# Feed-forward weights repacked into scratch DRAM by their first users, in a two-layer recurrent-memory transformer kernel

## The chip, the cores and the metric

One core of one Trainium2 chip runs the whole program. The metric is the device time of one execution in microseconds (us); lower is better. Times quoted as a median are of plain runs. The profile is of one further execution, with its own time.

## The reference, cut to what matters

Two layers of the same form run after each other on 2048 tokens of width 576. Attention goes through the tokens in 64 segments of 32, with 8 memory tokens handed from each segment to the next, so the segments of one layer can't be done at once. The feed-forward part has no such chain.

```
def _B_ref(x, w1, w3, w2):          # w1, w3: 576 x 4608, w2: 4608 x 576, bfloat16
    gate = jnp.einsum('bsd,df->bsf', x, w1)
    up = jnp.einsum('bsd,df->bsf', x, w3)
    h = _silu(gate) * up
    return jnp.einsum('bsf,fd->bsd', h, w2)

# A: 32 heads of 128, per segment: 8 memory tokens + 32 tokens, masked softmax, output projection;
#    the first 8 rows of a segment's output are the next segment's memory
x = x + _A_ref(_layernorm(x, axis=-1), A_mem0, A_Wq, A_Wk, A_Wv, A_Wo, A_seg_len)
x = x + _B_ref(_layernorm(x, axis=-1), B_w1, B_w3, B_w2)
# ... and the same two lines a second time, with the same weights
```

Both layers use the same weights.

## The kernel before

**Steps.** The program has 72 steps. Step `t` does segment `t` of the first layer and segment `t - 8` of the second, side by side where both exist, so the middle 56 steps are alike. A step goes through four groups of eight heads: projections (tiles `HT`, `W`, `QKT`), scores, softmax on VectorE and ScalarE (`SME`, `STAT`), the probabilities `PB`, their transposition to `PTS`, the product with `V`, and the output projection `WO`. In the middle steps the transposition is a DMA (`ptd`, the rows `PTS<-PB`). The tile `PB` has to be zeroed by GpSimd (`pb_zero`) before two of the four groups of each step.

**Jobs.** After every four steps a `job(j)` does the feed-forward part for 128 tokens of the first layer and 128 of the second (`ents` holds one or two of them). Its matrix products are laid between the attention of the next four steps. The hidden width of 4608 is cut into 18 units of 256 (`NPR = 18`), taken in pairs. Unit `pr` needs two blocks of weights: `W13` (256 columns of w1 and of w3: 576 KB) and `W2C` (256 rows of w2: 288 KB). The attention's weights stay in SBUF, so there is room for two `W13` slots and two `W2C` slots only, and every job loads all its units from the inputs again. That makes 302 loads of a unit: 18 in each of the jobs 0 to 15 and 14 in job 16. The last job's weights come in eight large pieces into the room that the attention's weights leave free (`tail_load`).

**Layouts.** w1 and w3 lie in DRAM as 576 rows of 4608, so a unit's `W13` is gathered from 1152 runs of 512 bytes. `load_w13` takes four DMAs for that: two of 128 x 4 x 256 elements and two of 64 x 256 (the last 64 of the 576 rows). `load_w2` is one DMA of 256 runs of 1152 bytes.

**Order.** TensorE's order is a string of letters (`ORDER`). The order on the other queues comes from `plan`, which goes through the nodes with estimated durations (a load: bytes / `dma_bw` and a latency) and picks at each point what can start first. A `Slot` is taken when its load is planned and comes free when all its `users` have released it. The emitted program keeps this order on each engine, and semaphores guard the data. All loads and the transpositions are issued by SyncE (SP) in one queue. GpSimd (POOL) zeroes `PB`, takes one power per layer norm (`LNS`), loads `XR` and stores the output.

Helpers record all operations, so many have one line: 653 is TensorE's, 666 ScalarE's, 669 VectorE's, 672 SP's plain loads, 687 GpSimd's DMAs, 1092 the zeroing of `PB`, 841 the power, 1095 the transposition.

Of the kernel before, what the change touches and what calls it, by code (L numbers as in the profile page):

```python
# [7 lines left out]
BF = mybir.dt.bfloat16  # L8
# [5 lines left out]
P = 128  # L14
# [225 lines left out]
    ustep, mode_pen, hor, wait, bulk, ff_split, last_win, tail_at = 0.0315, 0.1194, 0.0162, 0.141, 0.02, False, 2.5, -1.5  # L240


def make_nodes(em, nseg, pools, o=Opt, dma_bw=230e3, load_bw=400e3):

    ngrp = nseg // 4
    nodes = []
# [224 lines left out]
        return node("DVE", dve(576), em.post_add(li, g, xr[g], b[0]), deps=[d], prio=prio, rel=b, name="POSTa")  # L471

    last_up = []
    last_reads = [], []
    kept = {}

    def job(j):

        ents = [(0, j)] if 0 <= j < ngrp else []
        if 0 <= j - 2 < ngrp:  # L480
            ents.append((1, j - 2))
        if not ents:
            return
        s0 = 4 * j + 4 if j < ngrp else 4 * j - 4 + LAG
        ne = len(ents)
        last = s0 >= nst
        wr = []
        prev_ff = [] if last else list(last_up)
        cost = ewh(640)
        for (bi, g) in reversed(ents):  # L490
            pa = post(bi, g)
            wr += ln_nodes("F", xr[g], Slot("xn"), [pa], s0, [((lambda bi: lambda b: em.xtb_write(em.col(bi, g), b))(bi), cost, prev_ff)])
        w2_last = {}

        def finish(g, es):

            xn = Slot("xn")
            c = node("ACT", 0.574, em.fin_cast(xr[g], xn), deps=es, prio=s0 + LAG - 4.2, acq=[xn], rel=[xr[g]], name="fin")
            node("SWD", 1.0, em.store(g, xn), deps=[c], prio=s0 + LAG - 4.2, rel=[xn], lat=3.0, name="store")

        tail = None
        if last:
            v_done, qk_done = last_reads
            me = steps[nst - 1]
            rest = me["WO3"]
            pace = [(0, 2, me["SC1"]), (0, 3, me["PV0"]), (0, 4, me["WO1"]), (0, 1, me["WO1"]), (1, 2, me["PV3"]), (1, 3, rest), (1, 4, rest), (1, 1, rest),
                    (2, 2, rest), (2, 3, rest), (2, 4, rest), (2, 1, rest), (3, 2, rest), (3, 3, rest), (3, 4, rest), (3, 1, rest)]
            size = {1: kb(128, 8 * 576), 2: kb(128, 4 * 1024), 3: kb(128, 4 * 1024), 4: kb(128, 1024)}
            parts = {}
            for k, (i, what, after) in enumerate(pace):  # L510
                free = v_done if what == 1 else qk_done[4 * i:4 * i + 4]
                parts.setdefault(i, []).append(load("tail", size[what], s0 - 3.0 + 0.01 * k, em.tail_load(i, what, after), deps=free + [after]))
            tail = [parts[i // 2] for i in range(8)]

        npp = NPR // 2
        split = HELD if j == ngrp else 0
        own = ents
        if last:
            prev = [(1, own[0][1] - 1)]
            todo = [(pp, prev, 0.2 * pp - 1.0) for pp in range(HELD)] + [(pp, own, at) for at, pp in enumerate([npp - 1] + list(range(npp - 1)))]  # L520
        else:
            todo = [(pp, own, at) for at, pp in enumerate(range(split, npp))]
        for pp, ents, at in todo:
            mids, w2s, htts, lds = [], [], [], []
            stays = last and pp == npp - 1
            ne = len(ents)
            mm = (128 * ne / 2.4 + 2.5) / 1000
            for pr_ in (2 * pp, 2 * pp + 1):
                prio = s0 + o.ff + (o.win if s0 + 4 < nst else o.last_win) * (2 * at + pr_ % 2) / NPR
                if stays:  # L530
                    w13, w2 = kept[pr_]
                    ld = []
                    w2s.append(w2)
                elif last:
                    w13 = w2 = None
                    ld = tail[pp]
                else:
                    keep = s0 < nst <= s0 + 4 and pp == npp - 1
                    w13, w2 = Slot("w13", users=2 + keep), Slot("w2", users=ne + keep)
                    kept[pr_] = w13, w2  # L540
                    ld = [node("DMA", kb(1152, 256) / dma_bw, em.load_w13(pr_, w13), prio=prio - 1, acq=[w13], lat=2.3, name="W13")]
                    lds.append(node("DMA", kb(256, 576) / dma_bw, em.load_w2(pr_, w2), prio=prio - 0.99, acq=[w2], lat=2.2, name="W2l"))
                    w2s.append(w2)
                b = banks()
                if ne == 2 or pr_ % 2 == 0:
                    htt = Slot("htt", users=ne)
                at_ = em.htt_at(ents, pr_)
                rel13 = [w13] if w13 else []
                wd = ld if ents is not own else wr + ld
                fm = node("PE", 16 * mm, em.ffn_up(ents, pr_, w13, b, last and not stays, False), deps=wd, prio=prio, mode="full/col",  # L550
                          acq=b + [htt], rel=rel13, name="FF", wide=0.01)
                ff = node("PE", 2 * mm, em.ffn_up(ents, pr_, w13, b, last and not stays, True), deps=wd, prio=prio + o.fft, mode="row",
                          acq=b + [htt], rel=rel13, name="FFt")
                a = node("ACT", actc(256 * ne), em.ffn_tanh(ents, b, htt, at_), deps=[fm, ff], prio=prio - 0.5, name="tanh")
                c = node("DVE", 2 * dve(256 * ne) + 0.12, em.ffn_mul(ents, b, htt, at_), deps=[a], prio=prio - 0.5, rel=b, name="mul")
                last_up[:] = [fm, ff]
                mids.append(c)
                htts.append((htt, at_))
            for (bi, g) in ents:
                b = banks()  # L560
                used = list({id(h): h for h, _ in htts}.values()) + w2s
                at_bi = em.col(bi, g) * P if ne == 2 else 0
                if last and at == npp - 1:
                    d = node("PE", 4 * 0.1225, em.ffn_down(at_bi, pp, htts, w2s, b, True, (0,)), deps=mids[:1], prio=prio + o.w2,
                             mode="full/col", acq=b, name="W2b", wide=0.003)
                    mids = mids[1:] + [d]
                d = node("PE", (4 if last and at == npp - 1 else 8) * 0.1225, em.ffn_down(at_bi, pp, htts, w2s, b, last and not stays, (1,) if last and at == npp - 1 else (0, 1)),
                         deps=mids + lds, prio=prio + o.w2, mode="full/col", acq=b, rel=used, name="W2b" if bi else "W2", wide=0.005)
                if last and at == npp - 1:
                    xn = Slot("xn")  # L570
                    for h in (0, 1):
                        e_ = node("DVE", dve(288), em.fin_add(g, h, xr[g], xn, b[h]), deps=[d], prio=prio + o.w2, acq=[xn], rel=[b[h]], name="W2a")
                        node("SWD", 1.0, em.store_half(g, h, xn), deps=[e_], prio=s0 + LAG - 4.2, lat=2.0, name="store")
                    return
                es = [node("DVE", dve(288), em.ffn_add(g, h, xr[g], b[h]), deps=[d], prio=prio + o.w2, rel=[b[h]], name="W2a")
                      for h in (0, 1)]
                w2_last[bi] = es
                if last and ents is not own and pp == HELD - 1:
                    finish(g, es)
        for (bi, g) in own:  # L580
            if bi == 0:
                ht_set(1, g, ln_nodes("L1", xr[g], Slot("xn"), w2_last[0], s0 + LAG - 4.2, ht_writes(1, g)))
            elif not split:
                finish(g, w2_last[1])
# [43 lines left out]
class Emitter:  # L628
# [140 lines left out]
    def load_x(self, g, xr):  # L769
        return lambda n: self.swdma(self.T.XR[:, xr.i, :], self.a.x[g * P:(g + 1) * P, :])  # L770

    def load_w13(self, pr, w13):
        def f(n):
            fa = pr * 2 * P
            W = self.T.W13[:, w13.i]
            for kind, wd in ((0, self.a.w1), (1, self.a.w3)):
                self.dma(W[:, 4 * kind:4 * kind + 4], wd[0:4 * P, fa:fa + 2 * P].rearrange("(c p) f -> p c f", p=P))
            for kind, wd in ((0, self.a.w1), (1, self.a.w3)):
                self.dma(W[kind * R64:(kind + 1) * R64, 8], wd[4 * P:D, fa:fa + 2 * P])
        return f  # L780

    def load_w2(self, pr, w2):
        fa = pr * 2 * P
        return lambda n: self.dma(self.T.W2C[:, w2.i], self.a.w2[fa:fa + 2 * P, :].rearrange("(b p) d -> p b d", p=P))

    def tail_load(self, i, what, after):

# [529 lines left out]
def kernel(  # L1317
# [60 lines left out]
    T.W13 = sp.tile([P, pools["w13"], NCH, 2 * P], BF, name="W13")  # L1378
    T.W2C = sp.tile([P, pools["w2"], 2, D], BF, name="W2C")
    T.HTT = sp.tile([P, pools["htt"], 2, 2 * P], BF, name="HTT")  # L1380
    T.M0 = T.XTB[:].rearrange("p a b -> p (a b)")[:, 0:D]

    T.banks = [pp.tile([P, 512], F32, name=f"bank{i}") for i in range(pools["bank"])]
# [62 lines left out]
```

## Time and profile before

| | |
|---|---|
| median of 3 runs | 2625.83 us (2620.28 to 2628.71) |
| the profiled execution | 2624.02 us, of which the span is 2622.2 us |
| granted TensorE clock | 0.999 |
| TensorE (PE) busy | 2567.1 us, 98% of the span |
| VectorE (DVE), ScalarE (ACT), GpSimd (POOL) busy | 77%, 48%, 7% |
| SP's DMA queue (q1) | 353.23 MB, 52.5% of the time of 16 DMA engines |

How to read it: "A <- B" in a row of waits means that A stood idle until B had ended, with the total in us, the number of times and the longest; PEld is TensorE's loading of weights, and an engine's name with a q is its instruction queue. A row of DMA issues gives the size of one DMA and the median time from its issue to the landing of its data. In the program's names `W<-in_B_w_dram` stands for the loads of `W13` and of the last job's weights alike (the profile leaves numbers out of names).

### The profile page before, as it was taken

To read this page: it belongs to the slowest core of one execution; us is meant where nothing else is said; L and a number is where in the kernel's file an instruction comes from. 1 tells how busy PE (TensorE), PEld (TensorE's weight loads), DVE (VectorE), ACT (ScalarE), POOL (GpSimd) and SP (SyncE) were. 2 spreads that over 40 slices of the span, in tenths; PEclk is the share of its full clock that TensorE was granted. 3 is DMA by queue.
4 is the path that set the end of the run, shared out by engine and by line. 5 is a ranking of instruction groups with operands and counts; after the bars stand their busy time and mean duration, and the time that the engine had idled before them with its cause. 6 is when DMAs were issued, how large, how long until landed. Compare 5 with 4: busy or idle time off the path is not lost.

```text
span 2622.2 us, 131462 instructions
## 1 busy us (share of the span) xinstructions
PE 2567.1 (98%) x58447; PEld 2205.6 (84%) x58498; DVE 2009.5 (77%) x5145; ACT 1266.8 (48%) x3743; POOL 196.1 (7%) x253
## 2 busy tenths in 40 slices
PE   6999999999999999999999999999999999999998
PEld 4788888888888888888888888888888888888887
DVE  4778777787787688777867877786787778777877
ACT  2655453544545354454535445453544545445553
POOL 1100000000001000000000000010000000010000
PEclk9999999999999999999999999999999999999999
DMA  9064746565464656555465655546465554554447
GB/s 326 4 181 126 193 103 154 126 152 136 126 139 115 148 128 153 135 126 141 115 148 128 155 133 127 144 109 151 128 156 132 126 143 112 128 146 129 123 131 258
DMA packets 680217, 369.58 MB, mean 141 GB/s; under 512 B 233592, under 2 KB 669824, under 8 KB 679008
## 3 DMA queue, kind: packets, MB, share of 16 engines
q1 hardware_dynamic: 675968, 353.23, 52.5%
q8 instruction: 457, 7.49, 1.2%
q0 software_dynamic: 3024, 6.93, 0.9%
q10 hardware_dynamic: 656, 1.02, 0.2%
q14 instruction: 112, 0.92, 0.1%
HBM read 304.95 MB, written 2.36 MB: 117 GB/s over the span
## 4 chain that ended last, share of the span: by engine, by line
PE 90%; DMA 4%; DVE 3%; SPq 1%; issue 1%; ACT 1%; ACTq 0%; DVEq 0%
PE bank L653 90%; DMA PTS<-PB 2%; DMA W<-in_B_w_dram 1%; SPq L672 1%; DVE STAT L669 1%; DVE PB L669 1%; DVE SME L669 1%; DMA WV<-in_A_Wv_dram 0%; DVE HTT L669 0%; DMA W<-in_A_Wk_dram 0%; ACT V L666 0%; DVE V L669 0%; PE bank L663 0%; DMA W2C<-in_B_w_dram 0%; ACT HT L666 0%
## 5 line engine op out<-in xcount | busy, mean ns | idle before, releaser
L653 PEld LDWEIGHTS <-W 128*128 128x128 bf16 (+2 forms) x32096 | 1252.3, 100 | 121.3 <-issue 66.1
L653 PE MATMUL bank<-HT,W 128*128 128x80 bf16 (+3 forms) x23040 | 792.9, 197 | 9.6 <-ACT HT L666 5.4
L653 PE MATMUL bank<-XTB,W 128*64 128x256 bf16 (+5 forms) x9056 | 662.5, 264 | 4.5 <-DMA W<-in_B_w_dram 4.2
L666 ACT ACTIVATE QKT<-bank 128x192 bf16<-128x192 f32 (+4 forms) x1674 | 382.2, 312 | 274.5 <-PE bank L653 268.7
L653 PE MATMUL bank<-OT,WO 128*128 128x80 bf16 (+3 forms) x11520 | 411.1, 198 | 1.3 <-issue 1.3
L653 PEld LDWEIGHTS <-WO 128*128 128x128 bf16 (+1 forms) x11520 | 380.4, 102 | 27.6 <-issue 13.4
L666 ACT ACTIVATE V<-bank 64x512 bf16<-64x512 f32 (+1 forms) x589 | 333.0, 585 | 136.7 <-PE bank L653 129.8
L653 PE MATMUL bank<-WV,HT 128*32 128x512 bf16 (+4 forms) x3430 | 355.9, 381 | 6.8 <-issue 4.3
L653 PE MATMUL bank<-W2C,HTT 128*64 128x288 bf16 (+1 forms) x3152 | 322.1, 287 | 0.7 <-DMA W2C<-in_B_w_dram 0.6
L666 ACT ACTIVATE HTT<-bank 128x512 bf16<-128x512 f32 (+1 forms) x324 | 173.1, 550 | 284.0 <-PE bank L653 283.1
L669 DVE SCALAR_TENSOR_TENSOR XR<-bank,XR 128x288 f32<-128x288 f32 x574 | 243.4, 448 | 59.0 <-PE bank L653 53.4
L669 DVE TENSOR_REDUCE STAT<-SME 104x8 f32<-104x320 f32 (+1 forms) x576 | 273.8, 475 | 12.2 <-ACT SME L666 5.0
L669 DVE TENSOR_TENSOR PB<-SME,STAT 40x128 bf16<-40x128 f32 (+4 forms) x912 | 275.1, 336 | 8.1 <-issue 0.2
L653 PEld LDWEIGHTS <-HT 128*32 128x32 bf16 (+4 forms) x3472 | 147.5, 98 | 140.3 <-issue 24.9
L1092 POOL MEMSET PB<- 128x1024 bf16 x142 | 134.8, 951 | 1742.7 <-DMA PTS<-PB 1219.4
L653 PEld LDWEIGHTS <-HTT 128*64 128x64 bf16 (+1 forms) x3232 | 231.4, 105 | 35.7 <-issue 5.6
L669 DVE SCALAR_TENSOR_TENSOR HTT<-HTT,bank 128x512 bf16<-128x512 bf16 (+1 forms) x324 | 200.9, 620 | 69.7 <-ACT HTT L666 65.8
L666 ACT ACTIVATE OT<-bank 128x320 bf16<-128x320 f32 (+1 forms) x389 | 145.1, 402 | 203.8 <-PE bank L653 196.6
L669 DVE TENSOR_TENSOR HTT<-HTT,bank 128x512 bf16<-128x512 bf16 (+1 forms) x324 | 203.5, 628 | 28.0 <-DVE HTT L669 0.9
L666 ACT ACTIVATE SME<-SME 104x320 f32<-104x320 f32 (+1 forms) x288 | 135.0, 469 | 180.9 <-DVE SME L669 179.0
L669 DVE CAST V<-bank 64x512 bf16<-64x512 f32 (+1 forms) x275 | 188.3, 685 | 40.8 <-PE bank L653 36.4
L669 DVE TENSOR_TENSOR SME<-bank,maskb 104x320 f32<-104x320 f32 (+1 forms) x288 | 138.9, 483 | 39.4 <-PE bank L653 36.1
(61 smaller groups left out, 1400.8 us busy)
## 6 DMA issues: line engine op xcount, KB each, us to landing
W<-in_B_w_dram SPq DMA_DIRECT2D x604, 256.0 KB, 3.5
W2C<-in_B_w_dram SPq DMA_DIRECT2D x302, 288.0 KB, 3.5
W<-in_B_w_dram SPq DMA_DIRECT2D x604, 32.0 KB, 3.5
W<-in_B_w_dram SPq DMA_DIRECT2D x8, 1024.0 KB, 13.0
W<-in_A_Wq_dram SPq DMA_DIRECT2D x9, 512.0 KB, 9.9
WO<-in_A_Wo_dram SPq DMA_DIRECT2D x4, 1152.0 KB, 16.8
XR<-in_A_x_dram POOLq DMA_DIRECT2D x16, 288.0 KB, 2.9
WV<-in_B_w_dram SPq DMA_DIRECT2D x4, 1152.0 KB, 12.3
```

What stands on the lines that cost most here:

```text
L653: self.ch("PE", self.nc.tensor.matmul(out, lhsT=lhsT, rhs=rhs, start=start, stop=stop, skip_group_check=True, **k))
L666: self.ch("ACT", self.nc.scalar.activation(*a, **k))
L669: self.ch("DVE", getattr(self.nc.vector, fn_)(*a, **k))
L672: self.ch("SP", self.nc.sync.dma_start(out=out, in_=in_))
L1092: return lambda n: self.ch("POOL", self.nc.gpsimd.memset(self.pbt(pb), 0.0))
```

## The change

Each pair of units is written once to scratch DRAM tensors (`S13`, `S2`), in the very layout of the SBUF tiles: pair 0 (units 0 and 1) in job 1, pair 1 in job 2, and so on to pair 8 in job 9 (`save_in`). The job that writes a pair still loads it from the inputs; after the load has landed, GpSimd issues one software DMA for its `W13` and one for its `W2C`. In all later jobs the pair is loaded from the scratch tensors by SP: one DMA of 128 runs of 4608 bytes in place of the four for `W13`, and one of 128 runs of 2304 bytes for `W2C`. The slot of a unit that is being written has one user more, so it comes free only when the write has ended too. The planner is told a higher rate for the repacked loads (`pack_bw`).

```
+def save_in(pr):
+    return 1 + pr // 2
...
-                    w13, w2 = Slot("w13", users=2 + keep), Slot("w2", users=ne + keep)
+                    w13, w2 = Slot("w13", users=2 + keep + (j == save_in(pr_))), Slot("w2", users=ne + keep + (j == save_in(pr_)))
+                    bw = pack_bw if j > save_in(pr_) else dma_bw
...
-                    ld = [node("DMA", kb(1152, 256) / dma_bw, em.load_w13(pr_, w13), prio=prio - 1, acq=[w13], lat=2.3, name="W13")]
+                    ld = [node("DMA", kb(1152, 256) / bw, em.load_w13(pr_, w13, j), deps=saved.get(pr_, [])[:1], prio=prio - 1, acq=[w13], lat=2.3, name="W13")]
...
+                    if j == save_in(pr_):
+                        saved.setdefault(pr_, []).append(node("SWD", 1.0, em.save_w13(pr_, w13), deps=ld, prio=prio - 0.9, rel=[w13], lat=4.0, name="W13s"))
+                        saved.setdefault(pr_, []).append(node("SWD", 1.0, em.save_w2(pr_, w2), deps=lds[-1:], prio=prio - 0.9, rel=[w2], lat=4.0, name="W2s"))
...
-    def load_w13(self, pr, w13):
+    def load_w13(self, pr, w13, j):
         def f(n):
             fa = pr * 2 * P
             W = self.T.W13[:, w13.i]
+            if j > save_in(pr):
+                self.dma(W, self.T.S13[pr])
+                return
...
+    def save_w13(self, pr, w13):
+        return lambda n: self.swdma(self.T.S13[pr], self.T.W13[:, w13.i])
+
+    def save_w2(self, pr, w2):
+        return lambda n: self.swdma(self.T.S2[pr], self.T.W2C[:, w2.i])
...
+    dp = ctx.enter_context(tc.tile_pool(name="scratch", bufs=1, space=bass.MemoryType.DRAM))
+    T.S13 = [dp.tile([P, NCH, 2 * P], BF, name=f"S13_{i}") for i in range(NPR)]
+    T.S2 = [dp.tile([P, 2, D], BF, name=f"S2_{i}") for i in range(NPR)]
```

The rows on TensorE, VectorE and ScalarE are the same in both programs, one by one. SP and GpSimd have other rows. The first place is SP's queue in job 4, from a transposition on: `W_84` is the tile `W13`, `W2C` the other, and `S_5` and `S_4` are the scratch tensors of units 5 and 4. Before:

```order
L1095 DMA_TRANSPOSE PTS<-PB 128x8x112
L672 DMA W_84<-in_B_w_dram 128x4x256 x2
L672 DMA W_84<-in_B_w_dram 64x256 x2
L1095 DMA_TRANSPOSE PTS<-PB 128x8x112
L672 DMA W_84<-in_B_w_dram 128x4x256 x2
L672 DMA W_84<-in_B_w_dram 64x256 x2
L672 DMA W2C<-in_B_w_dram 128x2x576 x2
```

The same place in the changed program:

```order
L1114 DMA_TRANSPOSE PTS<-PB 128x8x112
L682 DMA W_84<-S_5_94 128x2304
L1114 DMA_TRANSPOSE PTS<-PB 128x8x112
L682 DMA W_84<-in_B_w_dram 128x4x256 x2
L682 DMA W_84<-in_B_w_dram 64x256 x2
L682 DMA W2C<-S_4_111 128x1152
L682 DMA W2C<-S_5_112 128x1152
```

Unit 5 comes in one DMA now; unit 6, which job 4 is to write, still comes in four. The transpositions keep their places between the units.

The second place is GpSimd's queue in the same job, from the load of `XR` on. Before:

```order
L687 DMA XR<-in_A_x_dram 128x576
L687 DMA out_dram<-XN 128x576
L1092 MEMSET PB 128x1024
L841 TENSOR_TENSOR LNS<-LNS,mhalf 128x1 x2
L1092 MEMSET PB 128x1024 x2
L841 TENSOR_TENSOR LNS<-LNS,mhalf 128x1
L1092 MEMSET PB 128x1024 x4
```

The same place in the changed program (`S_6_95` and `S_7_96` are the scratch tensors of `W13` for units 6 and 7, `S_6_113` and `S_7_114` those of `W2C`):

```order
L697 DMA XR<-in_A_x_dram 128x576
L697 DMA out_dram<-XN 128x576
L1111 MEMSET PB 128x1024
L860 TENSOR_TENSOR LNS<-LNS,mhalf 128x1 x2
L1111 MEMSET PB 128x1024 x2
L697 DMA S_6_95<-W_84 128x2304
L697 DMA S_7_96<-W_84 128x2304
L697 DMA S_6_113<-W2C 128x1152
L697 DMA S_7_114<-W2C 128x1152
L860 TENSOR_TENSOR LNS<-LNS,mhalf 128x1
L1111 MEMSET PB 128x1024 x4
```

Four writes stand now between the zeroing of `PB` and the next layer norm's power, and the power and the later zeroings are queued behind them.

More of the change, by code (lines that the diff above doesn't have):

```diff
@@ L240, with make_nodes @@
     ustep, mode_pen, hor, wait, bulk, ff_split, last_win, tail_at = 0.0315, 0.1194, 0.0162, 0.141, 0.02, False, 2.5, -1.5
-def make_nodes(em, nseg, pools, o=Opt, dma_bw=230e3, load_bw=400e3):
+def save_in(pr):
+    return 1 + pr // 2
+def make_nodes(em, nseg, pools, o=Opt, dma_bw=230e3, load_bw=400e3, pack_bw=350e3):
     ngrp = nseg // 4
@@ L473, in make_nodes @@
     last_up = []
+    saved = {}
     last_reads = [], []
@@ L538, in job @@
                     keep = s0 < nst <= s0 + 4 and pp == npp - 1
-                    w13, w2 = Slot("w13", users=2 + keep), Slot("w2", users=ne + keep)
+                    w13, w2 = Slot("w13", users=2 + keep + (j == save_in(pr_))), Slot("w2", users=ne + keep + (j == save_in(pr_)))
+                    bw = pack_bw if j > save_in(pr_) else dma_bw
                     kept[pr_] = w13, w2
-                    ld = [node("DMA", kb(1152, 256) / dma_bw, em.load_w13(pr_, w13), prio=prio - 1, acq=[w13], lat=2.3, name="W13")]
-                    lds.append(node("DMA", kb(256, 576) / dma_bw, em.load_w2(pr_, w2), prio=prio - 0.99, acq=[w2], lat=2.2, name="W2l"))
+                    ld = [node("DMA", kb(1152, 256) / bw, em.load_w13(pr_, w13, j), deps=saved.get(pr_, [])[:1], prio=prio - 1, acq=[w13], lat=2.3, name="W13")]
+                    lds.append(node("DMA", kb(256, 576) / bw, em.load_w2(pr_, w2, j), deps=saved.get(pr_, [])[1:], prio=prio - 0.99, acq=[w2], lat=2.2, name="W2l"))
                     w2s.append(w2)
+                    if j == save_in(pr_):
+                        saved.setdefault(pr_, []).append(node("SWD", 1.0, em.save_w13(pr_, w13), deps=ld, prio=prio - 0.9, rel=[w13], lat=4.0, name="W13s"))
+                        saved.setdefault(pr_, []).append(node("SWD", 1.0, em.save_w2(pr_, w2), deps=lds[-1:], prio=prio - 0.9, rel=[w2], lat=4.0, name="W2s"))
                 b = banks()
@@ L780, in load_w13, with load_w2 @@
         return f
-    def load_w2(self, pr, w2):
+    def load_w2(self, pr, w2, j):
         fa = pr * 2 * P
-        return lambda n: self.dma(self.T.W2C[:, w2.i], self.a.w2[fa:fa + 2 * P, :].rearrange("(b p) d -> p b d", p=P))
+        return lambda n: self.dma(self.T.W2C[:, w2.i], self.T.S2[pr] if j > save_in(pr) else self.a.w2[fa:fa + 2 * P, :].rearrange("(b p) d -> p b d", p=P))
+    def save_w13(self, pr, w13):
+        return lambda n: self.swdma(self.T.S13[pr], self.T.W13[:, w13.i])
+    def save_w2(self, pr, w2):
+        return lambda n: self.swdma(self.T.S2[pr], self.T.W2C[:, w2.i])
     def tail_load(self, i, what, after):
```

## Prediction

> **What bounds the kernel now.** I read the page's busy times and the chain that ended last first, to learn which engine sets the time.
>
> ```profile
> PE 2567.1 (98%) x58447; PEld 2205.6 (84%) x58498; DVE 2009.5 (77%) x5145; ACT 1266.8 (48%) x3743; POOL 196.1 (7%) x253
> q1 hardware_dynamic: 675968, 353.23, 52.5%
> PE 90%; DMA 4%; DVE 3%; SPq 1%; issue 1%; ACT 1%; ACTq 0%; DVEq 0%
> ```
>
> TensorE works 98% of the span. The DMA engines, which the change relieves, are busy for half of it and end 4% of the chain. So the change can save only what TensorE loses to DMAs. Next I took the waits of TensorE alone, in the stretch of jobs 2 to 9 (360 to 1584 us) and in that of jobs 10 to 16 (1584 to 2560 us). Columns: total us, times, longest.
>
> ```profile
> PE bank L653 <- ACT HT L666: 2.7, 8, 0.3
> PE bank L653 <- DMA PTS<-PB: 2.6, 4, 1.5
> PE bank L653 <- issue: 2.5, 16, 0.2
> PE bank L653 <- DMA W<-in_B_w_dram: 0.4, 1, 0.4
> ...
> PE bank L653 <- ACT HT L666: 2.4, 7, 0.3
> PE bank L653 <- issue: 2.2, 11, 0.6
> PE bank L653 <- DMA PTS<-PB: 1.1, 3, 0.5
> ```
>
> For the weights themselves TensorE waits 0.4 us in 2200. It waits longer, 2.6 + 1.1 us, for transpositions, which stand in the same SP queue behind the weights. To see whether more hides in the busy times I used the chain in order of time: the same piece of 83 instructions comes once in each job.
>
> ```profile
> 659.04 7.65 PE bank L653 x83
> ...
> 1117.29 7.65 PE bank L653 x83
> ...
> 1269.48 7.65 PE bank L653 x83
> ...
> 2187.24 7.65 PE bank L653 x83
> ```
>
> Ten jobs take 2187.24 - 659.04 = 1528.2 us, and the quickest of them 1269.48 - 1117.29 = 152.19. Were all like it, they would take 1521.9: 6.3 us are lost to stalls that come and go, 0.63 per job. From 360 to 2560 us, 14.4 such jobs, that is 9.1 us, of which 4.1 are the named waits. DMAs are the likeliest source of stalls that come and go, since the instructions of each job are alike.
>
> **The change: what it saves.** Pair p is written in job p + 1 and read from scratch in the jobs after it, to job 16 (which leaves out pairs 0 and 1): 14 + 13 + 13 + 12 + 11 + 10 + 9 + 8 + 7 = 97 pairs, 194 of the 302 units. Jobs 2 to 9 read 2, 4, ... 16 of their 18 units so, half on average; jobs 10 to 16 read all. The prices of a load and of its issues on SP:
>
> ```profile
> W<-in_B_w_dram SPq DMA_DIRECT2D x604, 256.0 KB, 3.5
> W2C<-in_B_w_dram SPq DMA_DIRECT2D x302, 288.0 KB, 3.5
> W<-in_B_w_dram SPq DMA_DIRECT2D x604, 32.0 KB, 3.5
> W<-in_B_w_dram SPq DMA_DIRECT2D x8, 1024.0 KB, 13.0
> XR<-in_A_x_dram POOLq DMA_DIRECT2D x16, 288.0 KB, 2.9
> out_dram<-XN POOLq DMA_DIRECT2D x15, 144.0 KB, 3.0
> ...
> L672 SPq DMA_DIRECT2D W2C<-in_B_w_dram x302: 368/419/1847, 52.6 to 2575.0; - x151
> ```
>
> And SP's queue in job 4, in order of time (start, us, what, how many):
>
> ```profile
> 685.07 2.79 SPq L672 DMA_DIRECT2D W<-in_B_w_dram  x4
> 688.03 1.22 SPq L1095 DMA_TRANSPOSE PTS<-PB  x1
> 689.35 2.29 SPq L672 DMA_DIRECT2D W<-in_B_w_dram  x4
> 693.19 1.24 SPq L1095 DMA_TRANSPOSE PTS<-PB  x1
> 694.54 2.26 SPq L672 DMA_DIRECT2D W<-in_B_w_dram  x4
> ...
> 700.93 3.74 SPq L672 DMA_DIRECT2D W<-in_B_w_dram  x4
> 704.76 1.25 SPq L1095 DMA_TRANSPOSE PTS<-PB  x1
> 706.11 2.28 SPq L672 DMA_DIRECT2D W<-in_B_w_dram  x4
> 708.49 1.04 SPq L672 DMA_DIRECT2D W2C<-in_B_w_dram  x2
> 709.63 9.04 SPq L672 DMA_DIRECT2D W<-in_B_w_dram  x8
> ```
>
> Four issues take 2.28 us of SP. One issue should take about what one `W2C` takes, 0.42. That frees 194 x 1.9 = 360 us of SP, but SP isn't the bound: it stands and waits for TensorE to free a slot, or for `PB`, between these rows. What is left of the gain is that a transposition behind a unit is issued some 1.9 us sooner. That is longer than any wait of TensorE for a transposition quoted above (longest 1.5). So I let the named waits go where units come from scratch: 0.5 x (2.6 + 0.4) + 1.1 = 2.6 us. If all 9.1 us of coming and going stalls shrink in the same proportion (half in 8 jobs, all in 6.4: 10.4 / 14.4), it is 6.6. I take 4.0, between the two and nearer to the named waits.
>
> Once these stalls are gone, the waits for ScalarE (`HT`) and "issue" are the next, and the change leaves them: the rows of TensorE, ScalarE and VectorE are the same in both programs. The first 360 us (jobs 0 and 1) and the last job's big loads read the inputs as before: 0 (the last job's longest wait is 2.2 us, which more room on the queue could take at most).
>
> **What it adds.** 36 software DMAs on GpSimd, each holding a slot until it has ended. Nothing in the trace writes 576 KB to DRAM; call the time from its issue to its landing T. The bounds are 2.9 us (`XR`, half the size) and 13.0 us (1024 KB, on a full queue). The nearest row is `XR`: 2.9 us, and its second half at the rate of the busy queue, 353.23 MB in 0.525 x 2622.2 us, or 257 KB per us: 295 KB take 1.15. The engines are half busy with loads besides, so I add about one more: T = 5.
>
> [...]
>
> How long may a write last? The SP rows show when a slot is free: unit u + 2 is loaded once unit u has been used. Between 685.07 and 694.54, 689.35 and 700.93, 694.54 and 706.11, 700.93 and 709.63 lie 9.5, 11.6, 11.6 and 8.7 us. The load takes 2.3 us of issues and, from the last of them, 3.5 to land: about 5.4. So 3.3 to 6.2 us are left for T before the slot is held longer than now. And TensorE's use of a unit takes 2.7 us, from the first start to the last end of these two rows of its timeline:
>
> ```profile
> 698.81 1.91 PE L653 MATMUL bank<-XTB,W 128*128 128x256 bf16 x16
> ...
> 700.92 0.61 PE L653 MATMUL bank<-XTB,W 64*128 64x256 bf16 x8
> ```
>
> So the next load has 8.7 - 5.4 - 2.7 = 0.6 to 11.6 - 8.1 = 3.5 us to spare. TensorE stops, then, where T is over 3.9 to 9.7 us, depending on the place. Spread evenly, a write costs (T - 3.9)^2 / 11.6 on average: 0.10 us at T = 5, and 18 writes of `W13` 1.9 us. The writes of `W2C` are half the size, near the lower bound 2.9: 0.
>
> Behind a write on GpSimd stand the zeroing of `PB` and the power of a layer norm. In job 4:
>
> ```profile
> 707.59 0.95 POOL L1092 MEMSET PB<- 128x1024 bf16 x1 [3.93 <-DMA PTS<-PB]
> 727.79 0.55 POOL L841 TENSOR_TENSOR LNS<-LNS,mhalf 128x1 f32<-128x1 f32 x1 [19.25 <-DVE LNS L669]
> ...
> L687 POOL DMA_DIRECT2D XR<-in_A_x_dram x16: 572/572/722, 55.3 to 2346.5; - x16
> ```
>
> GpSimd stands idle for 19.25 us ahead of this power. The loads of `W2C` for units 6 and 7 were issued after these 709.63 + 9.04 us of `W13`, so their landing and two issues of 0.57 us end about when the power is due; a delay of a us in one or two jobs is the worst that I see. I put it at 0.
>
> Last, the writes share the engines with the transpositions: 18 x 885 KB at 257 KB per us are 62 us of the queue in nine jobs of 153 us, so 4.5% of their 144 transpositions, some 6, land up to 2.3 us later. TensorE waited for 7 of some 220 in the table above; with a few that are close I count 0.3 us (0 to 6).
>
> **The sum,** against the profiled execution of 2624.0 us (2622.2 of span and 1.8 around it): 2624.0 - 4.0 + 1.9 + 0.3 = 2622.2. The median of the runs, 2625.83, lies 1.8 above the profiled execution, so as a median I say 2624.0. Its own range is 2617 (6.6 saved, the tail's 2.2 too, nothing paid) to 2632 (2.6 saved, T = 6.2: 8.2 paid, and 1 for the rest). A measurement of this kernel can tell about 0.3%, 7.9 us, from no change.
>
> **The rivals.**
>
> *All stalls that come and go vanish (faster).* If the queue is so much calmer that already the half-converted jobs run like the quickest, 9.1 us go, and 2.2 of the last job: 2624.0 - 11.3 = 2612.7, as a median 2614.5. For it: the named waits end with transpositions, and these stand behind four issues now. Against it: the packets stay, 885 KB per unit, and only 4.1 of the 9.1 us are named as DMA waits.
>
> *The writes hold the slots (slower).* The place is SP in jobs 1 to 9: it stands before the second load after a written unit until the write has ended, and the transpositions behind it stand too. Scaled from the 1024 KB row, T = 13.0 x 576 / 1024 = 7.3: each write costs 3.4^2 / 11.6 = 1.0 us, 18 of them 17.9, and the time is 2624.0 - 4.0 + 17.9 + 0.3 = 2638.2, as a median 2640.0. It decides from T = 6.7 on, where the cost, 12.2, outweighs the gain by over 7.9. For it: two slots, and spare times down to 0.6 us. Against it: all 31 software DMAs of before have medians of 2.9 and 3.0 us, and their issue takes 572 ns, 722 at the longest, beside a VectorE that is 77% busy.
>
> [...]
>
> *Nothing comes of it (no change).* Loads from scratch may land no sooner, if the 3.5 us are a latency: the 32 KB and the 256 KB loads have the same 3.5. Then only the costs stay: 2624.0 + 2.2 = 2626.2, as a median 2628.0.
>
> **How the numbers follow.** My forecast 0.48, no gain 0.12: both within 7.9 us of 2625.83. Stalls vanish 0.20: faster. Writes hold the slots 0.20: slower. The range reaches to the centres of the two outer rivals, 2613 to 2640, since half of each lies beyond its centre and 2 in 10 may be left out.
>
> **What would show it.** Right: TensorE's waits for `PTS` after 1584 us fall from 1.1 us towards 0, the quickest job is still 152.2 us, writes of 576 KB land in about 5 us, and SP's new rows issue in about 0.4. Wrong: jobs 10 to 16 at the same pace as before (no gain), jobs quicker than 152.2 (a loss that I don't see), or waits of TensorE for `W` in jobs 1 to 9 of over 5 us, with writes of 7 us or more (the slower rival).

## The result, and the profile after

The changed kernel takes 2635.96 us (median of 11 runs, 2627.25 to 2646.42), the kernel before beside it on the same chip 2626.31 (11 runs): a ratio of 1.0038, with a 95% interval of 1.0022 to 1.0053. It is slower, by 6 to 14 us; the forecast was no change. The profiled execution of the changed kernel, 2627.25 us (span 2625.4), is the quickest of its 11, so its rows show the new queues and prices, but little of the loss.

The page, the rows that answer to those of before:

```profile
PE 2569.3 (98%) x58447; PEld 2204.2 (84%) x58498; DVE 2009.5 (77%) x5145; ACT 1266.3 (48%) x3743; POOL 216.5 (8%) x289
q1 hardware_dynamic: 443168, 353.19, 50.8%
q0 software_dynamic: 7056, 22.86, 2.5%
PE 87%; DMA 5%; DVE 5%; issue 1%; SPq 1%; ACT 1%; ACTq 0%; POOL 0%; DVEq 0%
```

The same bytes come in a third fewer packets (before 675968), and SP's queue is nearly as full as before (52.5%). The waits of TensorE, again from 360 to 1584 us and from 1584 to 2560:

```profile
PE bank L663 <- issue: 3.6, 17, 1.0
PE bank L663 <- DMA PTS<-PB: 2.9, 7, 0.7
PE bank L663 <- ACT HT L676: 2.7, 8, 0.3
PE bank L663 <- DMA W2C<-in_B_w_dram: 0.7, 2, 0.4
...
PE bank L663 <- issue: 3.7, 13, 0.8
PE bank L663 <- ACT HT L676: 2.4, 7, 0.3
PE bank L663 <- DMA PTS<-PB: 1.3, 3, 0.9
```

The waits for `PTS` have not gone: 2.9 and 1.3 us, where before had 2.6 and 1.1, although all units after 1584 us come from scratch. The waits put down to "issue" have grown, from 2.5 and 2.2 us to 3.6 and 3.7. The DMA issues (KB, median us to landing), with SP's and GpSimd's prices of an issue (min/median/max ns):

```profile
W<-S SPq DMA_DIRECT2D x194, 576.0 KB, 4.3
W2C<-S SPq DMA_DIRECT2D x194, 288.0 KB, 3.5
W<-in_B_w_dram SPq DMA_DIRECT2D x216, 256.0 KB, 4.0
S<-W POOLq DMA_DIRECT2D x18, 576.0 KB, 4.9
S<-W2C POOLq DMA_DIRECT2D x18, 288.0 KB, 4.7
...
L682 SPq DMA_DIRECT2D W<-S x194: 319/325/1507, 328.6 to 2569.5; - x194
L697 POOL DMA_DIRECT2D S<-W x18: 531/582/582, 209.2 to 1558.1; - x18
```

A unit's `W13` costs SP one issue of 0.33 us in place of four, and a write of 576 KB lands 4.9 us after its issue: the prices of the forecast (0.4 and 5). One of 288 KB takes nearly as long, 4.7. The piece of 83 instructions in the chain, in jobs 10 to 14:

```profile
1575.28 7.65 PE bank L663 x83
...
2184.83 7.65 PE bank L663 x83
```

Four jobs take 609.55 us, against 1576.51 to 2187.24, 610.73, before: they are 0.3 us per job quicker in this execution. From the last of these pieces to the end of the span it is the other way round: 2625.4 - 2184.83 = 440.6 us, against 2622.2 - 2187.24 = 435.0 before. What was found there stands under "Do the loads bring anything?".

### The profile page after: what moved, and what is told of

It reads as the page before. It is cut to its first block, busy times and chain, and to the rows that moved or that the text cites. A ratio compares the mean times of both kernels' runs of the same rounds, so it can differ in the third digit from the quotient of the medians.

```text
span 2625.4 us, 130575 instructions
## 1 busy us (share of the span) xinstructions
PE 2569.3 (98%) x58447; PEld 2204.2 (84%) x58498; DVE 2009.5 (77%) x5145; ACT 1266.3 (48%) x3743; POOL 216.5 (8%) x289
## 4 chain that ended last, share of the span: by engine, by line
PE 87%; DMA 5%; DVE 5%; issue 1%; SPq 1%; ACT 1%; ACTq 0%; POOL 0%; DVEq 0%
PE bank L663 87%; DMA PTS<-PB 3%; DVE STAT L679 1%; DVE PB L679 1%; DMA W<-in_B_w_dram 1%; DVE HTT L679 1%; DVE SME L679 1%; SPq L682 1%; DMA W<-in_A_Wk_dram 1%; DMA WV<-in_A_Wv_dram 0%; DMA W2C<-in_B_w_dram 0%; DVE V L679 0%; DMA WV<-in_B_w_dram 0%; DVE XR L679 0%; ACT V L676 0%
```

## The experiments

All ratios are to the kernel before, run beside it on the same chip, with a 95% interval. Only SP's and GpSimd's queues differ between these programs; TensorE, VectorE and ScalarE have the rows of before in all of them. The edits are cut to the lines that matter; they start from the changed kernel. `pack_bw` is 230e3 besides, so that SP's loads and transpositions stand in the order of before, in all but four: the first with loads only, the change unhooked, with `W13` in four DMAs, and in 5 pieces.

### Writes or loads?

**Writes only:** all 302 loads from the inputs again, and what is written is read by nobody.

```
-            if j > save_in(pr):
-                self.dma(W, self.T.S13[pr])
-                return
```

> The 36 writes of the change are made, but nobody reads them: all 302 units come from the inputs as before. Burst theory (a repacked load puts 576 KB on the engines with one issue, and transpositions and TensorE's instruction loads queue up behind it): no bursts here, so within 0.1% of before, ratio 0.999 to 1.001. Write theory (the writes hold the two slots and share the engines in jobs 1 to 9): the whole loss, ratio 1.003 to 1.005, and TensorE's waits for W between 200 and 1584 us are over 5 us.

Measured 1.0033 (1.0020 to 1.0046): nearly the whole loss of the change. The theory that bursts of repacked loads are the main cause falls. The waits for `W` of over 5 us, by which the theory of writes was to be known, didn't come either: from 360 to 1584 us they are 1.2.

**Loads only:** no writes; the same 194 units come in runs of 4608 and 2304 bytes from contiguous pieces of the inputs.

```
-                self.dma(W, self.T.S13[pr])
+                wd = (self.a.w1, self.a.w3)[pr % 2]
+                self.dma(W, wd[pr // 2 * R64:(pr // 2 + 1) * R64, :].rearrange("r (h c) -> (r h) c", h=2))
```

> No scratch and no writes: the same 194 units are loaded by one DMA of 128 runs of 4608 bytes and one of 128 runs of 2304 bytes, but from contiguous pieces of the inputs (so the weights of those units are permuted; only the time is of interest). Burst theory: most of the loss is still there, ratio 1.002 to 1.004, TensorE's idle time put down to issue is over 11 us (9.4 before), and transpositions land in a median of over 3.2 us. Write theory: ratio 0.997 to 1.000, since only the gain is left.

Measured 1.0010 (1.0001 to 1.0019). No gain, although TensorE hardly waits for `PTS` between 360 and 1584 us of the profiled execution:

```profile
PE bank L660 <- DMA PTS<-PB: 0.5, 2, 0.3
```

One execution says little here: in the run "loads only, in SP's order of before", further down, the same waits are 3.9 us.

**The change, unhooked:** the writes take their bytes from `WO`, so they hold no slot, and GpSimd waits for no load.

```
-        return lambda n: self.swdma(self.T.S2[pr], self.T.W2C[:, w2.i])
+        return lambda n: self.swdma(self.T.S2[pr], self.T.WO[:, 4:6, :])
```

> As the change, but the 36 writes take their bytes from the output projection's tile, which nobody waits for: a slot has no third user, and GpSimd waits for no load (so the scratch holds other values; only the time is of interest). If holding the slots is what costs: ratio 0.998 to 1.000. If it is the traffic of the writes or the bursts of the loads: ratio 1.002 to 1.005, as with the change.

Measured 1.0027 (1.0017 to 1.0036): the slot that a write holds is at most a part of the loss.

**The change, `W13` from scratch in four DMAs:**

```
-                self.dma(W, self.T.S13[pr])
+                for k in range(4):
+                    ks = slice(k * D, (k + 1) * D)
+                    self.dma(W.rearrange("p a b -> p (a b)")[:, ks], self.T.S13[pr][:].rearrange("p a b -> p (a b)")[:, ks])
```

> As the change, but a W13 from scratch comes in four DMAs of 128 runs of 1152 bytes, issued one after the other. Burst theory: SP paces the load again (4 issues of about 0.35 us), so about half of the loss goes, ratio 1.000 to 1.003, and the idle time put down to issue is below the 12.8 us of the change. Write theory: as with the change, ratio 1.003 to 1.005.

Measured 1.0032 (1.0021 to 1.0043): the pace of the loads makes no difference that can be told from the change's 1.0038. The trace of the writes-only kernel, in order of time, shows what a write does:

```profile
1395.04 2.86 SPq L1111 DMA_TRANSPOSE PTS<-PB  x1
1395.35 0.54 POOL L697 DMA_DIRECT2D S<-W  x1 [7.51 <-DMA W<-in_B_w_dram]
1402.36 0.46 PE L663 MATMUL bank<-PTS,V 128*128 128x80 bf16 x8 [2.21 <-DMA PTS<-PB]
```

SP issues a transposition right behind the loads of a unit. GpSimd has waited 7.51 us for a load to land and issues its write 0.31 us after the transposition. TensorE then idles for 2.21 us. The times from issue to landing in this run (min/median/max), first of the transpositions from 360 to 1584 us, then of all DMAs with the scratch tensors, here the writes:

```profile
DMA to landing us min/median/max: 2.6/3.0/7.1
...
DMA to landing us min/median/max: 3.1/4.6/6.8
```

The longest write is this one: it lands at 1395.35 + 6.8 = 1402.1. The trace has no landing for this transposition, but TensorE, which waits for it, starts at 1402.36, 7.3 us after its issue and just behind the write's landing. The longest transposition with a landing, 7.1 us, is another one: it is issued at 892.86 us, 0.3 us ahead of a write of a `W2C`, and lands at 900.0, the write at 899.8. So a transposition, 3.0 us at the median, has landed with the write beside it, twice. 111 transpositions of 360 to 1584 us have a landing. Grouped by whether a write was in flight beside them for half a microsecond or more, with the mean from issue to landing, they are 14 with a write at 5.06 us and 97 others at 3.28.

How many packets of the write went before the transposition, the trace doesn't show.

### Bytes, or GpSimd's queue?

**Tiny writes:** as writes only, each cut to 64 bytes per partition.

```
-        return lambda n: self.swdma(self.T.S13[pr], self.T.W13[:, w13.i])
+        return lambda n: self.swdma(self.T.S13[pr][:, 0, 0:32], self.T.W13[:, w13.i, 0, 0:32])
```

> As the kernel with writes only (all 302 loads from the inputs, nobody reads what is written), but each write carries 64 bytes per partition, 8 KB in place of 576 or 288 KB: the same 36 software DMAs at the same places in GpSimd's queue, with the same waits, and about a sixtieth of the bytes. Traffic theory (the bytes of a write delay the transposition issued beside it): 1.000, no more than 1.001, waits for PTS back near 4 us, no single one of 2 us or more. Queue theory (what costs is that GpSimd issues and waits, whatever the bytes): 1.003 as with the full writes. [...]

Measured 0.9998 (0.9989 to 1.0007). **Each write twice:**

```
+        return lambda n: [self.swdma(S[pr], self.T.W13[:, w13.i]) for S in (self.T.S13, self.T.S13B)]
```

> As the kernel with writes only, but each tile is written twice, into two scratch tiles: 72 software DMAs in place of 36, 31 MB in place of 15.5. Traffic theory: the loss over before grows from 0.33% to between 0.5 and 0.8%: a transposition that lands near the write meets twice the bytes, and the half-clock stretches of 3.41 us that follow the longest waits come more often. Coincidence theory (the loss is a small fixed cost of another program, not of the bytes): 1.003 still.

Measured 1.0117 (1.0101 to 1.0133), over three times the loss, and more than the 0.5 to 0.8% expected. Together with the tiny writes: the bytes cost, and not the DMAs as such. TensorE's waits for `PTS` from 360 to 1584 us, in the kernels with whole, tiny and double writes:

```profile
PE bank L663 <- DMA PTS<-PB: 6.1, 7, 2.2
...
PE bank L663 <- DMA PTS<-PB: 1.7, 4, 0.5
...
PE bank L663 <- DMA PTS<-PB: 21.9, 13, 4.3
```

**All writes in job 0,** before the first transposition by DMA: the change with `save_in` at 0, so that 284 units come from scratch, and with a planner that isn't told of the held slots.

```
-    return 1 + pr // 2
+    return 0
```

> The change with all 36 writes in job 0 (save_in gives 0), which ends before the first transposition by DMA at about 246 us; 284 units come from the scratch tiles. The planner isn't told that a write holds a tile, so that the order on TensorE, ScalarE and VectorE stays that of before. Traffic theory (writes cost through the transpositions beside them, and there are none here): 1.001, the level of the kernel with repacked reads only (0.9995 to 1.0025 for 284 units at its interval); job 0 itself may lose 1 to 3 us to the tiles that the writes hold, which would show before 270 us. Theory of the bytes as such (writes cost wherever they lie): 1.003 to 1.004.

Measured 1.0091 (1.0076 to 1.0106), worse, for another reason. TensorE's and SP's waits from 130 to 250 us, and that stretch (the last three numbers: granted clock, share of the DMA engines, GB/s):

```profile
PE bank L663 <- DMA W<-in_B_w_dram: 12.2, 11, 4.0
...
SPq L682 <- DMA S<-W: 45.1, 10, 6.1
...
130.00:250.00 120.00, 103.78 (x2692) 86.14 (x2689) 77.74 (x213) 53.72 (x151) 25.21 (x42) 0.91 0.80 256
```

With 18 units written in one job SP waits 45.1 us for slots and TensorE 12.2 for weights, at a clock of 0.91. Before had 0.8 us of such waits there, at a clock of 0.99. Here the rival of the held slots is seen at work; in the change, with two units per job, it isn't. From 360 to 1584 us, with no write beside the transpositions, TensorE waits 1.4 us for `PTS` in this trace (before 2.6).

### Pieces, and the moment

**13 pieces:** writes only, from `WO` (no slot held, no load waited for), 9 pieces of 64 KB and 4 of 72 per unit.

```
+                        for k in range(NCH):
+                            node("SWD", 1.0, em.save_w13(pr_, k), deps=ld, prio=prio - 0.9, lat=4.0, name="W13s")
```

> Writes only (nobody reads them, all 302 loads from the inputs), from a tile that is never overwritten (no tile is held), each unit's 576 and 288 KB cut into 9 pieces of 64 KB and 4 of 72 KB, which GpSimd issues some 0.55 us apart: the same bytes at 120 GB/s or less, 234 software DMAs. Traffic theory, if the burst counts: 1.000 to 1.0015, with no wait for PTS of 2 us or more. Traffic theory, if only the sum of bytes counts: 1.002 to 1.003. Queue theory: GpSimd issues for 7 us per unit, over 120 us in all, and its LNS powers and PB memsets come up to 0.6 us late: 1.004 or more.

Measured 0.9997 (0.9988 to 1.0005). **The same with whole writes,** `range(1)`:

> Writes only (nobody reads them), from a tile that is never overwritten, each whole: 36 DMAs of 576 or 288 KB. It differs from the writes in 13 pieces (0.9997) in the number of pieces alone, and from the first writes-only kernel (1.0033) in that no tile is held. Burst theory: 1.002 to 1.003, with single waits for PTS of 2 us or more behind a write. Theory that holding a tile is what cost, and the pieces were free because they held none: 1.000.

Measured 1.0017 (1.0007 to 1.0027): half the loss, without the long waits for `PTS` (360 to 1584 us):

```profile
PE bank L665 <- DMA PTS<-PB: 2.7, 5, 0.8
```

Where this half goes, its trace doesn't show. **The same in 5 pieces,** `range(3)` and `range(2)`:

> As the last, each unit's 576 KB in 3 pieces of 192 and its 288 in 2 of 144, which GpSimd issues some 0.55 us apart, so that they come at over 250 GB/s, about as fast as a whole write. If what counts is the rate at which the bytes come: 1.0015 to 1.003, near the whole writes. If what counts is the size of one DMA (a transposition gets in between two pieces): 1.000 to 1.001, as with 13 pieces.

Measured 1.0001 (0.9991 to 1.0011). **The change, copied from the inputs,** DRAM to DRAM, in 14 pieces per unit:

```
+            return lambda n: self.swdma(self.T.S13[pr][:, k], (self.a.w1, self.a.w3)[k // 4][k % 4 * P:(k % 4 + 1) * P, fs])
```

> The change in another form: the scratch tiles are filled from the inputs themselves, DRAM to DRAM, in 10 pieces of 64 or 32 KB and 4 of 72 KB per unit, at the places where the change writes its tiles; no tile of SBUF is held or read for it, and 194 units come from scratch as in the change. Burst theory (a whole write delays the transposition beside it, pieces don't) with a gain of the repacked loads as in the trace of the kernel with repacked reads only (4.2 us between 529 and 2139 us): 0.9985, faster than before. Burst theory with no gain of the loads (that kernel's median): 1.000 to 1.001. If the bytes count whatever their pieces: 1.002 to 1.004, with the extra reads of DRAM on top.

Measured 1.0010 (0.9999 to 1.0021), with no slot held and no load waited for: the loss of the change is gone for the most part, and a gain hasn't come. After these I held that the size of one write decides. **5 pieces from the unit's own tile,** which is what the change would write, took that down:

```
-        return lambda n: self.swdma(self.T.S13[pr], self.T.W13[:, w13.i])
+        return lambda n: [self.swdma(self.T.S13[pr][:, 3 * k:3 * k + 3], self.T.W13[:, w13.i, 3 * k:3 * k + 3]) for k in range(3)]
```

> The first writes-only kernel (1.0033: all 302 loads from the inputs, nobody reads what is written), its writes from the unit's own tile, which is held until the last piece has landed, and after its load, but each in 3 pieces of 192 KB or 2 of 144. Burst theory (a whole write beside a transposition is all that cost): 1.000 to 1.001, waits for PTS near 4 us with none of 2 us. Slot theory (holding the tile carries about half): 1.0015 to 1.002, with waits for W above 3 us between 360 and 1584 us.

Measured 1.0043 (1.0027 to 1.0060). **The change itself in these 5 pieces:**

> The change itself, with each W13 write in 3 pieces and each W2C write in 2, nothing else: it computes the reference from the scratch tiles. Burst theory: the change's 1.0038 falls to 1.000 to 1.001, the level of the repacked loads alone (0.9998 and 1.001). If the loss is in holding the tile or in the loads and writes together: 1.002 to 1.004.

Measured 1.0038 (1.0023 to 1.0052), the loss of the change. Its timeline:

```profile
543.11 0.58 POOL L697 DMA_DIRECT2D S<-W  x1 [18.77 <-DMA W<-in_B_w_dram]
543.61 1.41 SPq L1114 DMA_TRANSPOSE PTS<-PB  x1
543.86 1.07 POOL L697 DMA_DIRECT2D S<-W  x2 [0.17 <-DMA W<-in_B_w_dram]
...
551.59 0.46 PE L663 MATMUL bank<-PTS,V 128*128 128x80 bf16 x8 [3.06 <-DMA PTS<-PB]
```

The pieces go out within 1.82 us and are one burst. So either the held slot costs, or the moment: hooked writes, those from the unit's own tile, follow a load, and that is when SP issues the next transposition. Transpositions that met a write, counted as above: 17 in the hooked kernel in 5 pieces, 7 in the unhooked one. Two runs parted these. **A tile held without bytes,** 8 and 4 tiny writes one after the other:

```
+        return lambda n: [self.swdma(self.T.S13[pr][:, k, 0:32], self.T.W13[:, w13.i, k, 0:32]) for k in range(8)]
```

> The tiny writes (0.9998), but 8 of them for each W13 tile and 4 for each W2C tile, one after the other, 8 KB each: the tile is held for some 7 us after its load, longer than by a whole write of 576 KB (4.6 us), and about 2% of the bytes move. Slot theory, by the prediction's own formula for a hold of 7 us ((7 - 3.9) squared over 11.6, 0.8 us per tile, 18 tiles): 15 us, 1.006; at the least 1.002. Burst theory: 1.000, within 0.001.

Measured 1.0018 (1.0008 to 1.0028), between the two, and the trace names a third cause:

```profile
222.73 4.25 POOL L697 DMA_DIRECT2D S<-W  x8 [6.20 <-DMA W<-in_B_w_dram]
227.00 0.58 POOL L857 TENSOR_TENSOR LNS<-LNS,mhalf 128x1 f32<-128x1 f32 x1
227.61 0.58 DVE L679 TENSOR_SCALAR XN<-XR,LNS 128x576 bf16<-128x576 f32 x1 [1.77 <-POOL LNS L857]
228.25 0.50 PE L663 MATMUL bank<-ident,XN 128*128 128x128 bf16 x5 [1.61 <-DVE XN L679]
```

Eight issues keep GpSimd for 4.25 us, the layer norm's power stands behind them, VectorE waits for the power and TensorE for VectorE. From 300 to 2560 us TensorE has no wait of over 0.9 us in this run, although SP waits 13.1 us for held `W13` tiles from 360 to 1584 us, so the held tile itself shows no price. **Whole writes after the load, the tile let go early:** a tiny write of the unit's tile, which waits for the load, and behind it the whole bytes from `WO`.

```
+        return lambda n: (self.swdma(self.T.SB[2 * pr], self.T.W13[:, w13.i, 0, 0:32]),
+                          self.swdma(self.T.S13[pr][:].rearrange("p a b -> p (a b)"), self.T.WO[:, 0:4, :].rearrange("p a b -> p (a b)")))
```

> Writes only: at the place of each write of the change a tiny write of the unit's own tile (8 KB, which waits for its load and holds the tile as the tiny writes did, which lost nothing), and right behind it the whole 576 or 288 KB from a tile that is never overwritten. The moment and the bytes are those of the first writes-only kernel (1.0033), the tile is held no longer than by the tiny writes (0.9998). Theory of the moment: 1.003, single waits for PTS of 2 us or more near 550 and 1400 us. Slot theory: 1.000 to 1.0017.

Measured 1.0036 (1.0025 to 1.0048), the loss of writes only. SP's waits for held tiles from 360 to 1584 us, in writes only and here, and TensorE's for `PTS` here:

```profile
SPq L682 <- DMA S<-W: 11.9, 5, 6.2
...
SPq L682 <- DMA SB<-W2C: 0.6, 1, 0.6
...
PE bank L663 <- DMA PTS<-PB: 7.3, 8, 2.2
```

SP hardly waits for a held tile any more, 0.6 us in all, and the loss stays. From the whole unhooked writes (1.0017) this kernel differs in the moment, and in tiny writes that cost nothing: by this pair the moment makes about half of the loss. What the other half is stays open: cut in 5 pieces, the unhooked writes lost nothing (1.0001), and the hooked ones all (1.0043). **13 pieces from the unit's own tile:**

> Writes only, from the unit's own tile and after its load as in the change, 9 pieces of 64 KB and 4 of 72 KB: the tile is held for about 8 us, and the bytes come 0.55 us apart in small pieces. Theory of the moment (a transposition that meets a burst lands with it): pieces of 64 KB leave less ahead of a transposition than 576 KB do, so 1.001 to 1.003, with waits for PTS between those of the tiny writes (1.7 us in 360 to 1584 us) and of the whole ones (6.1). Slot theory: no less than 1.0043, the writes in 5 pieces, since the tile is held longer.

Measured 1.0045 (1.0029 to 1.0061), more than I expected. Its waits for `PTS` are between the others as expected (4.2 us, longest 1.0), but GpSimd's queue costs again, in the same place as above:

```profile
221.55 4.79 POOL L697 DMA_DIRECT2D S<-W  x9 [8.38 <-DMA W<-in_B_w_dram]
226.36 0.58 POOL L858 TENSOR_TENSOR LNS<-LNS,mhalf 128x1 f32<-128x1 f32 x1
...
227.60 0.45 PE L663 MATMUL bank<-ident,XN 128*128 128x128 bf16 x5 [2.20 <-DVE XN L679]
```

The wait is 2.20 us; how much of the loss (medians of 2631.70 and 2621.68 us) comes from GpSimd's queue wasn't tried apart.

### Do the loads bring anything?

**Loads only, in SP's order of before** (`pack_bw=230e3`):

> Repacked reads only, no writes, as the run that gave 1.001, but the planner's speed for these loads stays at 230 KB/us in place of 350, so that SP's loads and transpositions stand in the order of before. The units read contiguous pieces of the inputs, not the feed-forward's own values. If the order of SP's queue cost what the loads gained: 0.998 to 0.999. If the gain in the one trace was chance, or lost to something else: 1.000 to 1.001 again.

Measured 0.9998 (0.9988 to 1.0007). **284 units in long runs, no writes** (`save_in` at 0):

> Repacked reads only, no writes, for all units of jobs 1 to 15, 284 in place of 194 (contiguous pieces of the inputs, not the feed-forward's own values), in SP's order of before. If long runs save the waits for PTS and W, as the prediction had it (4.0 us for 194): 0.998 to 0.999. If the waits only come and go from run to run and long runs save nothing: 1.000, within 0.001.

Measured 1.0002 (0.9992 to 1.0013). At the forecast's rate, 4.0 us for 194, these 284 units would have given 5.9 us, 0.9978: outside the interval. The transpositions of 360 to 1584 us, from issue to landing, in before and in loads only in SP's order of before:

```profile
DMA to landing us min/median/max: 2.6/3.0/5.6
...
DMA to landing us min/median/max: 2.6/3.4/6.9
```

SP is free sooner, but the transposition lands later, by 0.4 us at the median. With `W13` in four DMAs of shorter runs it was 3.2 and the writes' loss no smaller, so this explains a part at most.

The long runs have a price at one place, which no run took apart. Near 2560 us, between the same instructions, TensorE waits in before and in the changed kernel:

```profile
2558.06 0.38 PE L653 MATMUL bank<-HT,W 128*128 128x40 bf16 x9 [0.56 <-issue]
...
2562.46 0.25 PE L663 MATMUL bank<-HT,W 128*128 128x40 bf16 x4 [1.84 <-issue]
```

In the changed kernel the granted clock is then at one half from 2564.0 to 2567.4 us. The instructions around this place, 25.0 us in before, take 27.1 to 27.9 us in seven of the eight traces in which a unit's `W13` comes in long runs by one DMA (in the eighth, loads only in SP's order of before, 25.2), and 24.8 to 25.5 in the 11 others, the one with `W13` from scratch in four DMAs among them. So some 2 to 3 us go here, and a gain elsewhere must make up for them first. What TensorE waits for there, the profile doesn't name.

## Why the prediction was wrong

**The step that failed is "the writes share the engines with the transpositions",** 0.3 us (0 to 6). Measured alone, writes after their loads cost 0.33% and 0.36%, 9 us, nearly all of what the change loses. Three things in it were too small. The count: some 6 of 144 transpositions, taken as if writes and transpositions met by chance; 14 of 111 met, since a write begins when its load lands, and SP issues a transposition right behind the loads. The delay: at most 2.3 us, the write's share of a queue; it was 1.8 us on average (5.06 for 3.28) and 4.3 at 1395.04 us (7.3 for 3.0), as long as the write lasts. And what TensorE loses by it: with a few close ones 0.3 us were counted, and its waits for `PTS` from 360 to 1584 us grew by 3.5 us in writes only (6.1 for 2.6) and by 4.7 in "whole writes after the load" (7.3). After some of the stalls TensorE runs at half clock for 3.4 us more, which the sum left out: between 360 and 2500 us five of the traces with writes have one to three such stretches, those of the change and of writes only none. With up to 1.7 us for a stretch (half of 3.41, an estimate), that names 3.5 us of the 9 in writes only, whose profiled execution is the quickest of its five, and 6.4 in the other; where the rest goes, these traces don't show.

**The gain of 4.0 us failed too,** in the way of the rival "Nothing comes of it", which foresaw that loads from scratch land no sooner. Three runs without writes give 1.0010, 0.9998 and 1.0002. I had taken the difference between the quickest job and the mean of one execution for stalls that the loads cause. Single executions do show less waiting (0.5 us for `PTS` from 360 to 1584 us in one, 3.9 in another, 2.6 in before), and in the medians no gain is left. The prediction also had the change leave the waits put down to "issue" as they were; in its trace they grew, and the one at 2562.46 us with the half clock behind it takes back more than half of a gain of 4.0. The packets, which were taken to stay, fell by a third, and nothing came of that.

**The slots** were put at 1.9 us. The runs show no price: T was 4.9 as assumed, and the loss stays where SP hardly waits for a held tile (1.0036 for 1.0033). In the changed kernel SP does stand for held tiles from 360 to 1584 us, 11.5 us for `W13` and 3.6 for `W2C`, but TensorE waits there for `W2C` for 0.7 us, and for `W13` not at all. "The writes hold the slots" wasn't the cause; that it gave the sign and nearly the size was luck. Only with all writes in one job does it decide. GpSimd's issues of the writes took about as long as those of the loads of `XR` before (572 to 722 ns): 531 to 582 ns for 576 KB, and 544 to 734 for 288 KB, where the median is 544.

**GpSimd's queue** at 0 was right for one issue per tile (tiny writes: 0.9998) and would have been wrong for eight.

**SP's issues** were right: 0.33 us for 0.4. They freed time on a queue that wasn't the bound.

## What to carry to other kernels

A transfer taken on to save another is to be priced at the moment at which it starts, and against the small urgent transfer of that moment: of two DMAs issued 0.3 us apart the small one landed with the large one, in the two cases that were followed. An average share of a queue doesn't give that, since whatever starts the one (a load that lands, a queue that comes free) starts the other too. And before a load is made cheaper, run it cheaper without its price, here loads without writes: that bounds the gain before anything is built for it.

## What was not expected of the hardware

After some of the stalls the trace's record of TensorE's granted clock is at one half for 3.41 us, then full again. The stretch behind the stall of 2.22 us at 393.41 us in the run "whole writes after the load" (the clock is the third number from the end):

```profile
393.41 0.69 PE L663 MATMUL bank<-PTS,V 128*64 128x80 bf16 x16 [2.22 <-DMA PTS<-PB]
...
393.50:396.90 3.40, 3.40 (x60) 3.31 (x61) 1.82 (x7) 1.12 (x3) 0.94 (x2) 0.50 0.99 244
```

In 3.41 us at half clock TensorE can do what takes 1.7 us at the full one, so by my estimate a stall of 2.2 us costs up to 1.7 us again. Behind the one of 2.11 us at 552.70 in the change with `W13` from scratch in four DMAs the clock is 0.50 from 553.4 to 556.8 us too. Not each stall has this price: the one of 3.06 us at 551.59 in the change in 5 pieces was followed by no such stretch. In before the stretches at full clock between such stretches are 719 and 2 times 3.41 us long, in the changed kernel 17 times. Counted in steps of 3.41 us from the changes of the clock in each trace, that stall is split between two steps (1.9 and 1.1 us), and the one of 2.22 us lies in a single step. In the 20 traces, leaving out both ends, each step at full clock in which TensorE idled for more than 2.0 us had half clock behind it; of those with less, up to 1.96 us, some had and some hadn't: in before 1.48 us in the step at 150.33 us had, 1.54 at 1317.69 hadn't, and in the changed kernel 1.84 at 2560.58 had. What sets this, no run here shows.
